# Block attention and expert router on one core: the second product of full expert tiles as seven block products in the two column halves of the array

## The chip, the core and the metric

The kernel runs on one core of a Trainium2 chip. The metric is device time in microseconds (us) of one execution; the lower the better. The engines are called PE (TensorE matmuls; PEld are its weight loads), DVE (VectorE), ACT (ScalarE), POOL (GpSimd) and SP (SyncE, which here issues DMAs).

## What is computed

A block-sparse attention gives x, 3072 rows of 512. Each row goes to the one of 8 experts whose embedding is nearest by cosine, and through that expert's two layers:

```python
N, D, E, F = (3072, 512, 8, 1024)
...
expert_idx = np.argmax(logits, axis=1)
...
for e in range(E):
    mask = expert_idx == e
    ...
    h = np.maximum(x[mask] @ w1[e], 0.0)
    out[mask] = gate_w[mask, None] * (h @ w2[e])
```

Everything is fp32. w1 of an expert is 512 x 1024, w2 1024 x 512: 2 MB each.

## The kernel before

The program has two stages. The first, written in a fixed order, does attention, the logits and most of the routing. The second works through 25 expert tiles of 128 rows (`expert_tiles`, tiles 0 to 24); the change lies in it. The order of instructions in this stage comes from a scheduler that places each engine's instructions from their dependencies and its own estimates of cost; a few places pin an order with `issue_after`. [...]

Tiles 0 to 4 (`NE` is 5) are made of rows that an early dispatch has sorted, the others of rows of the late dispatch. Tiles 11 and 17 are mixed: the upper and the lower 64 rows belong to two experts (`mixed_tile`), so they need two pairs of weights, and each column half of the PE array gets its own. The other 23 tiles are full (`expert_tile`, L1177).

A full tile does this:

- The first product (L1187): hidden features by rows, `h` transposed, in 8 blocks of 128 features, each a sum of 4 matmuls with the weights `w1` stationary and the rows `xt` (128 columns) moving. Blocks 0 to 3 go to PSUM bank `hp0`, blocks 4 to 7 to `hp4`; both have two copies, used in turn by even and odd tiles. An fp32 matmul stands in the profile as two instructions, so the 32 matmuls count 64.
- The relu of `hp0` by ACT (L1190), that of `hp4` by DVE (L1194) into `h`.
- `prepare` of the next tile: for a late tile one DVE transpose (L1168) of the rows fetched, then the gate factor (L1171, L1173); it is pinned to come after the relu (`k.relu`). For tiles 1 to 4 four PE transposes into the bank `xg_ps` and one DVE copy (L1163, L1164).
- The second product (L1200): 8 matmuls with the blocks of `h` stationary and `w2` (512 columns) moving, summed in the bank `yp`.
- `finish`: DVE multiplies `yp` by the gate into `y` (L1212), and POOL scatters `y` to the output rows (L1213). The gathers of a later tile's rows (four per late tile, L1111) are pinned behind that scatter on POOL.

SP loads the weights of each tile afresh (L1140). w1 and w2 have three buffers each; a load into a buffer waits till PE has done with it, so the loads run up to three tiles ahead. In PSUM this stage uses two banks each for `hp0` and `hp4`, one for `yp` and one for `xg_ps`; two more (`small`) serve the dispatch.

Of the kernel before, what the change touches and what calls it, by code (L numbers as in the profile page):

```python
# [16 lines left out]
ALU = mybir.AluOpType  # L17
# [3 lines left out]
P = 128  # L21
# [8 lines left out]
DM, E, F = H * D, 8, 1024  # L30
ND, NF = DM // P, F // P
# [4 lines left out]
HG = G // 2  # L36
# [18 lines left out]
NS = NCH // DUO  # L55
TURNS = [0, 2, 1, 3, *range(4, NCH)]
DEN_LOW, DEN_HIGH = 0.1, 1e10
NEG = -1.0e9
NONE = -30000.0

# [96 lines left out]
def block_mask(k):  # L157
# [16 lines left out]
    both = pool.tile([NB, NB], F32, name="both")  # L174
    nc.vector.tensor_scalar(out=both, in0=m, scalar1=1.0, scalar2=-NEG, op0=ALU.subtract, op1=ALU.mult)
    return both
# [905 lines left out]
def ring(k, name, i, n, pool, shape):  # L1082

    key = name, i % n
    if key not in k.rings:
        k.rings[key] = pool.tile(shape, F32, name=f"{name}_{i % n}")
    return k.rings[key]
# [10 lines left out]
def fetch_rows(k, i):  # L1098

    late = int(i >= NE)  # L1100
    x = ring(k, "xg", i, 4, k.wp2 if i % 4 else k.wp, [P, ND, XE])
    t = ORDER[i - NE] if late else i
    slot = k.slots[late][:, t:t + 1]
    with ExitStack() as order:
        behind = k.scattered if late else None
        if behind is not None:
            order.enter_context(k.tc.issue_after(behind))
        if late:
            quarters = k.x_dram.rearrange("n (e w) -> (n e) w", e=ND)
            for g in range(NG):  # L1110
                k.nc.gpsimd.indirect_dma_start(  # L1111
                    out=x[:, g], out_offset=None, in_=quarters,
                    in_offset=bass.IndirectOffsetOnAxis(ap=k.quarter[:, g, t:t + 1], axis=0),
                    bounds_check=quarters.shape[0] - 1, oob_is_err=False,
                )
        else:
            k.nc.gpsimd.indirect_dma_start(
                out=x.rearrange("p e w -> p (e w)"), out_offset=None, in_=k.x_dram[0:EARLY * S, :],
                in_offset=bass.IndirectOffsetOnAxis(ap=slot, axis=0), bounds_check=EARLY * S - 1, oob_is_err=False,
            )  # L1120
    k.rows[i] = x, slot
# [33 lines left out]
def prepare(k, i):  # L1155

    nc = k.nc
    x, slot = k.rows[i]
    turned = k.turned_rows[i] = ring(k, "xgt", i, 2, k.wp2 if i % 2 else k.wp, [P, ND, P])
    if i < NE:  # L1160
        ps = ring(k, "xg_ps", i, 1, k.eps, [P, ND, P])
        for d in range(ND):
            nc.tensor.transpose(ps[:, d, :], x[:, d, 0:P], k.ident)  # L1163
        nc.vector.tensor_copy(out=turned, in_=ps)  # L1164
        k.rows[i] = x[:, 0, P:XE], slot
        return
    with k.tc.issue_after(k.relu) if k.relu is not None else ExitStack():
        nc.vector.transpose(out=turned.rearrange("p d (g t) -> p d g t", g=NG),  # L1168
                            in_=x[:, :, 0:P].rearrange("p g (t d) -> p d g t", d=ND))
        own = ring(k, "own", i, 2, k.wp2, [P, NG])  # L1170
        nc.vector.tensor_tensor(out=own, in0=x[:, :, P], in1=k.mine, op=ALU.mult)  # L1171
        gate = ring(k, "gate", i, 3, k.wp2, [P, 1])
        nc.vector.reduce_sum(out=gate, in_=own, axis=AX.X)  # L1173
    k.rows[i] = gate, slot


def expert_tile(k, i, meanwhile=None, halfway=None, then=None):  # L1177
    nc = k.nc
    ((w1, w2),), (gate, slot) = k.weights.pop(i), k.rows.pop(i)
    xt = k.turned_rows.pop(i)  # L1180
    h = ring(k, "h", i, 2, k.wp2, [P, NF, P])
    half = NF // 2
    for f0 in (0, half):
        hp = ring(k, f"hp{f0}", i, 2, k.hps, [P, half, P])
        for f in range(half):
            for d in range(ND):
                nc.tensor.matmul(hp[:, f, :], lhsT=w1[:, d, (f0 + f) * P:(f0 + f + 1) * P], rhs=xt[:, d, :],  # L1187
                                 start=(d == 0), stop=(d == ND - 1))
        if f0 == 0:
            nc.scalar.activation(h[:, 0:half], hp, ACT.Relu)  # L1190
            if meanwhile:
                meanwhile()
        else:
            k.relu = nc.vector.tensor_scalar(out=h[:, half:NF], in0=hp, scalar1=0.0, scalar2=None, op0=ALU.max).ins  # L1194

    if i + 1 < k.stop:
        prepare(k, i + 1)
    yp = ring(k, "yp", i, 1, k.eps, [P, DM])
    for f in range(NF):
        nc.tensor.matmul(yp, lhsT=h[:, f, :], rhs=w2[:, f, :], start=(f == 0), stop=(f == NF - 1))  # L1200
        if f == half - 1 and halfway:
            halfway()
    if then:
        then()
    finish(k, i, yp, gate, slot)


def finish(k, i, yp, gate, slot):

    nc = k.nc  # L1210
    y = ring(k, "y", i, 2, k.wp2, [P, DM])
    nc.vector.tensor_scalar(out=y, in0=yp, scalar1=gate, scalar2=None, op0=ALU.mult)  # L1212
    k.scattered = nc.gpsimd.indirect_dma_start(  # L1213
        out=k.out[:, :], out_offset=bass.IndirectOffsetOnAxis(ap=slot, axis=0),
        in_=y[:, :], in_offset=None, bounds_check=N - 1, oob_is_err=False,
    ).ins


def mixed_tile(k, i):
# [29 lines left out]
    for f in range(NF):  # L1249
        for s, (_, w2) in enumerate(weights):  # L1250
            lanes = slice(HG * s, HG * (s + 1))
            nc.tensor.matmul(yp[lanes, :], lhsT=h[:, f, lanes], rhs=w2[:, f, :], start=(f == 0), stop=(f == NF - 1))  # L1252
    finish(k, i, yp, gate, slot)


# [279 lines left out]
def fast(n):  # L1535
    n.rings, n.loads = {}, 0
    with ExitStack() as ctx:
        def pool(name, bufs, **kw):
            return ctx.enter_context(n.tc.tile_pool(name=name, bufs=bufs, **kw))

        n.small, n.eps = pool("small", 1, space=PSUM), pool("eps", 1, space=PSUM)
        n.xp, n.rp, n.xt_pool = pool("xp", 3), pool("rp", 2), pool("xt", 2)
        n.wp_ctx = ctx
        with ExitStack() as attn:
            n.attending = True
            with n.tc.manual_schedule(engines=None):
                attention_fast(n, attn)
            n.attending = False
        n.dp = pool("dp", 1, reuse_waits="tile")
        n.wp2, n.hps = pool("wp2", 1, reuse_waits="tile"), pool("hps", 1, space=PSUM)  # L1550

        def last_rank():
            rank(n, B - 1)
            n.late = dispatch_late(n)
            next(n.late)

        def between():
            yield
            yield
            next(n.late)  # L1560
            count_good(n)
            yield

        def last_route():
            last_logits(n, NCH - 1)
            with n.tc.issue_after(n.relu):
                for _ in route(n, NS - 1):
                    pass

        for _ in n.first_weights:  # L1570
            pass
        for steps in n.unwritten:
            for _ in steps:
                pass
        fetch_rows(n, 1)
        expert_tiles(n, between(), partial(turn_x, n, NCH - 1), last_route, last_rank, lambda: next(n.late))


def more(n):
# [41 lines left out]
@with_exitstack  # L1621
def kernel(
    ctx: ExitStack,
    tc: tile.TileContext,
    q: bass.AP,
    k: bass.AP,
    v: bass.AP,
    sampled_blocks: bass.AP,
    moe_expert_emb: bass.AP,
    moe_tau: bass.AP,  # L1630
    moe_w1: bass.AP,
    moe_w2: bass.AP,
    out: bass.AP,
):
    assert tuple(q.shape) == (B, H, S, D) and tuple(out.shape) == (N, DM)
    assert tuple(moe_w1.shape) == (E, DM, F) and tuple(sampled_blocks.shape) == (NB, NRAND)
    n = Net()
    n.tc, n.nc = tc, tc.nc
    n.q, n.k, n.v, n.blocks, n.out = q, k, v, sampled_blocks, out
    n.emb, n.tau, n.w1, n.w2 = moe_expert_emb, moe_tau, moe_w1, moe_w2  # L1640
    n.loaded, n.vs, n.es, n.ets, n.sums, n.x, n.rows, n.weights = {}, {}, {}, {}, {}, {}, {}, {}

    n.raw, n.nsq, n.lg, n.turned_rows, n.relu = {}, {}, {}, {}, None
    n.kt, n.qt, n.kg, n.pac, n.pd, n.pb, n.av, n.xt = ({} for _ in range(8))
    n.exact = n.attending = False
    n.const = ctx.enter_context(tc.tile_pool(name="const", bufs=1))
    n.x_dram = tc.dram_tile([N + 1, XW], F32, name="x_dram")
    n.dens = n.const.tile([P, NCH, H], F32, name="dens")

    fast(n)  # L1650
    todo = n.nc.values_load(n.todo[0:1, 0:1], min_val=0, max_val=2)
    with tc.If(todo > 0):
        more(n)
# [32 lines left out]
```

## Time and profile before

| | |
|---|---|
| three runs | 632.02, 627.16, 631.42 us; median 631.42 |
| the profiled execution | 626.4 us, its span 624.7 us |
| clock granted to PE in it, mean | 0.986 |
| start of the first expert tile's matmuls | 257.1 us into the span |
| DMA: moved, mean rate | 170.58 MB, 273 GB/s |
| weight loads of the second stage | 52 of 2048 KB, 8 of 512 KB |

The profile is of one execution. Its page gives each engine's busy time and share of the span, the chain of waits that ended last (followed back from the last instruction), and groups of instructions by line: engine, operation, output<-input, shape, count, then busy us and the mean ns of one, then the engine's idle time before them and who ended it. Matmuls overlap in the array, so the mean duration of one is longer than the time from one to the next, and their ends are modelled. The groups of the second product and the scatter:

```profile
L1200 PE MATMUL yp<-w,h 128*128 128x512 f32 x368 | 161.9, 592 | 0.0
L1213 POOL DMA_INDIRECT out_dram<-y,slot_l x20 | 20.4, 1022 | 156.0 <-DVE y L1212 156.0
L1212 DVE TENSOR_SCALAR y<-yp,gate 128x512 f32<-128x512 f32 x20 | 15.0, 751 | 82.0 <-PE yp L1200 69.9
```

### The profile page before, as it was taken

The page shows a single profiled execution, that of the slowest core. Times are in us where ns is not written, and L with a number is a line of the kernel's source. Part 1 is how long each engine was busy: PE and PEld are TensorE (multiplying, and loading weights), DVE is VectorE, ACT ScalarE, POOL GpSimd, SP SyncE. Part 2 cuts the span into 40 slices and gives each one's busy share as a digit, 9 for nine tenths or more (in the row PEclk, how much of TensorE's full clock was granted, in tenths as well). Part 3 has the DMA queues.
Part 4 walks back from the last instruction along what each step waited for, and adds up shares of the span by engine and source line. Part 5 has one row for each costly group of instructions (what it writes and reads, how often), then busy time and mean ns, then how long its engine had stood idle before and what let it go on. Part 6 is the DMA issues. An engine that isn't in the chain of part 4 may idle for free.

```text
span 624.7 us, 18708 instructions
## 1 busy us (share of the span) xinstructions
PE 591.9 (95%) x7678; PEld 454.1 (73%) x7678; DVE 236.1 (38%) x745; ACT 148.0 (24%) x309; POOL 244.1 (39%) x474
## 2 busy tenths in 40 slices
PE   6789998989999997999999999999999999999995
PEld 3678887878888886967777667765777646777772
DVE  2636565676778853239212211212111221111110
ACT  1435555655656653200000000000000000000000
POOL 2626464555766430320243333343333333333432
PEclk9789999999999999999999999999999999999998
DMA  9889888999987971599999999998999998999611
GB/s 167 171 184 193 180 174 180 195 195 208 202 183 186 190 222 37 179 372 399 399 407 398 393 397 365 333 318 305 385 408 398 396 381 308 400 394 410 241 35 34
DMA packets 187312, 170.58 MB, mean 273 GB/s; under 512 B 147720, under 2 KB 147848, under 8 KB 184402
## 3 DMA queue, kind: packets, MB, share of 16 engines
q1 hardware_dynamic: 179906, 155.35, 80.2%
q0 software_dynamic: 5216, 13.43, 5.9%
q8 instruction: 62, 1.02, 0.7%
q10 hardware_dynamic: 2096, 0.52, 0.5%
q14 instruction: 32, 0.26, 0.1%
HBM read 156.65 MB, written 12.90 MB: 271 GB/s over the span
## 4 chain that ended last, share of the span: by engine, by line
PE 82%; ACT 5%; DMA 3%; DVE 2%; issue 2%; POOL 1%; SPq 0%; DVEq 0%; POOLq 0%; ACTq 0%
PE hp L1187 25%; PE yp L1200 24%; PE av L646 8%; PE dps L591 6%; PE ac L566 3%; PE ac L569 3%; PE hp L1232 2%; PE yp L1252 2%; DMA w<-in_moe_w_dram 2%; ACT st L458 2%; ACT pd L596 2%; PE xg_ps L723 2%; PE yp L530 1%; PE xg_ps L752 1%; ACT pb L624 1%
## 5 line engine op out<-in xcount | busy, mean ns | idle before, releaser
L1187 PEld LDWEIGHTS hp<-xgt,w 128*128 128x128 f32 x1472 | 167.8, 192 | 11.9 <-issue 10.2
L1187 PE MATMUL hp<-xgt,w 128*128 128x128 f32 x1472 | 169.2, 276 | 1.4 <-DMA w<-in_moe_w_dram 1.4
L1200 PE MATMUL yp<-w,h 128*128 128x512 f32 x368 | 161.9, 592 | 0.0
L1200 PEld LDWEIGHTS yp<-w,h 128*128 128x128 f32 x368 | 68.1, 190 | 76.5 <-issue 75.7
L1111 POOL DMA_INDIRECT xg<-x_dram,quarter x88 | 89.2, 1014 | 32.3 <-issue 27.4
L1213 POOL DMA_INDIRECT out_dram<-y,slot_l x20 | 20.4, 1022 | 156.0 <-DVE y L1212 156.0
L1190 ACT ACTIVATE h<-hp 128x512 f32<-128x512 f32 x23 | 13.7, 597 | 284.7 <-PE hp L1187 253.8
L1194 DVE TENSOR_SCALAR h<-hp 128x512 f32<-128x512 f32 x23 | 15.9, 691 | 148.5 <-PE hp L1187 148.5
L506 POOL COPY vg<-vt 32x1040 f32<-32x1040 f32 (+1 forms) x45 | 42.8, 952 | 45.6 <-PE av L646 34.4
L548 POOL COPY kg<-kt 128x128 f32 x176 | 43.7, 296 | 35.1 <-ACT kt L519 31.1
L591 PEld LDWEIGHTS dps<-qt,kg 128*64 128x64 f32 x1408 | 47.2, 140 | 3.4 <-issue 3.4
L591 PE MATMUL dps<-qt,kg 128*64 128x64 f32 x1408 | 46.3, 224 | 3.2 <-DVE kg L548 3.2
L566 PE MATMUL ac<-qt,kt 128*64 128x128 f32 x352 | 43.9, 277 | 3.0 <-DVE qt L535 2.7
L1212 DVE TENSOR_SCALAR y<-yp,gate 128x512 f32<-128x512 f32 x20 | 15.0, 751 | 82.0 <-PE yp L1200 69.9
L569 PE MATMUL ac<-qt,kt 128*64 128x256 f32 (+1 forms) x192 | 43.2, 368 | 0.9 <-ACT kt L522 0.9
L566 PEld LDWEIGHTS ac<-qt,kt 128*64 128x64 f32 x352 | 37.8, 137 | 4.2 <-issue 3.2
L535 DVE COPY qt<-yp 64x512 f32<-64x512 f32 x48 | 33.0, 688 | 20.7 <-PE yp L530 20.4
L596 ACT ACTIVATE pd<-dps,bias 128x256 f32<-128x256 f32 x88 | 34.7, 474 | 17.9 <-PE dps L591 17.9
L646 PE MATMUL av<-st,pac 128*64 128x65 f32 x704 | 31.2, 226 | 4.1 <-DVE x L841 3.4
L646 PEld LDWEIGHTS av<-st,pac 128*64 128x64 f32 x704 | 25.6, 138 | 8.6 <-issue 7.6
L646 PE MATMUL av<-vg,pd 128*32 128x65 f32 x1408 | 30.0, 225 | 1.8 <-issue 1.8
L725 DVE COPY xt<-xg_ps 128x512 f32<-128x512 f32 x24 | 16.6, 691 | 35.6 <-PE xg_ps L723 35.6
(240 smaller groups left out, 617.3 us busy)
## 6 DMA issues: line engine op xcount, KB each, us to landing
w<-in_moe_w_dram SPq DMA_DIRECT2D x52, 2048.0 KB
vg<-in_v_dram SPq DMA_DIRECT2D x132, 128.0 KB
kraw<-in_k_dram SPq DMA_DIRECT2D x32, 192.0 KB
x_dram<-x SPq DMA_DIRECT2D x10, 516.0 KB
qraw<-in_q_dram SPq DMA_DIRECT2D x9, 512.0 KB
w<-in_moe_w_dram SPq DMA_DIRECT2D x8, 512.0 KB
vt<-in_v_dram SPq DMA_DIRECT2D x10, 256.0 KB
vt<-in_v_dram SPq DMA_DIRECT2D x5, 512.0 KB
```

Source lines behind the costliest of these rows:

```text
L506: k.nc.gpsimd.tensor_copy(out=k.vg_ring[s % 2][lanes_of(NRAND, g), g, which(i)], in_=k.vt[m][rows, which(i)])
L535: k.nc.vector.tensor_copy(out=t[rows, :, h], in_=ps[rows])
L548: copy(out=t[:, :, g, lanes_of(s, g)], in_=kt[:, :, bass.ds(shift, BLK)])
L566: nc.tensor.matmul(out[0:D, j, half], lhsT=kt[:, j, at:at + D], rhs=qt[:, j, :, D * half:D * (half + 1)], start=True, stop=True)
L569: nc.tensor.matmul(out[D:P, j, half:2].rearrange("p f h t -> p h f t"), lhsT=kt[:, j, S:S + D], rhs=qt[:, j, :, D * half:P].rearrange("p h ...
L591: nc.tensor.matmul(out[D * r:D * (r + 1), NG * j + g], lhsT=kg[:, j, g, D * r:D * (r + 1)], rhs=qt[:, j, :, cols], start=True, stop=True)
L596: nc.scalar.activation(e[:, :, g].rearrange("p j h t -> p j (h t)"), out.rearrange("p (j g) h t -> p j g (h t)", g=NG)[:, :, g], ACT.Exp, ...
L646: k.nc.tensor.matmul(av[lanes, h // NPAIR, h % NPAIR * P:h % NPAIR * P + D + 1], lhsT=lhsT, rhs=rhs, start=first[0], stop=last, skip_group ...
L1111: k.nc.gpsimd.indirect_dma_start(out=x[:, g], out_offset=None, in_=quarters, in_offset=bass.IndirectOffsetOnAxis(ap=k.quarter[:, g, t:t + ...
L1187: nc.tensor.matmul(hp[:, f, :], lhsT=w1[:, d, (f0 + f) * P:(f0 + f + 1) * P], rhs=xt[:, d, :], start=(d == 0), stop=(d == ND - 1))
L1200: nc.tensor.matmul(yp, lhsT=h[:, f, :], rhs=w2[:, f, :], start=(f == 0), stop=(f == NF - 1))
L1213: k.scattered = nc.gpsimd.indirect_dma_start(out=k.out[:, :], out_offset=bass.IndirectOffsetOnAxis(ap=slot, axis=0), in_=y[:, :], in_offse ...
```

## The change

For the full tiles from 3 on, except the last (24), the second product is done by a form of Strassen's identity. The 128 rows of the tile are cut into top and low (64 each), the 1024 features into two halves, the 512 outputs into left and right. The product of two 2 x 2 block matrices is then seven products of blocks, p1 to p7, instead of eight. Each is 64 rows by 256 outputs, a sum over 4 blocks of 128 features, and occupies one column half of the array: p1, p2, p5 the lower-numbered half, p7, p4, p6 the other, in the pairs (p1, p7), (p5, p6), (p2, p4); p3 is cut in two sums over 2 blocks each, one in each half.

The blocks that go in are sums: `sums_of_weights` forms t1 to t4 of w2 on DVE (four operations of 128 x 1024; t1 is written over a part of w2 itself), and `expert_tile` s1 to s4 of h (`hsums`, four of 128 x 256). The results are put together from PSUM by DVE adds of 64 x 256 (u, v, w and parts of y), one such add on POOL, and ACT copies of p1 and p5 into both partition halves; the gate is applied by two ACT multiplies. For the products' outputs the change uses the banks `hp0` and `hp4` of the other parity, which the next tile's first product will write, and `yp` and `xg_ps`. The scatter gets a function of its own.

```diff
@@ -55,6 +55,7 @@
 NS = NCH // DUO
 TURNS = [0, 2, 1, 3, *range(4, NCH)]
 DEN_LOW, DEN_HIGH = 0.1, 1e10
+FIRST_SUMS = 3
 NEG = -1.0e9
 NONE = -30000.0
 
@@ -1174,12 +1175,81 @@
     k.rows[i] = gate, slot
 
 
+def sums_of_weights(k, i, w2):
+
+    nc, half = k.nc, NF // 2
+    left, right = slice(0, DM // 2), slice(DM // 2, DM)
+    t2, t3, t4 = (ring(k, f"wsum{j}", 0, 1, k.wp2, [P, half, DM // 2]) for j in (2, 3, 4))
+    nc.vector.tensor_tensor(out=t3, in0=w2[:, half:NF, right], in1=w2[:, 0:half, right], op=ALU.subtract)
+    t1 = w2[:, 0:half, right]
+    nc.vector.tensor_tensor(out=t1, in0=t1, in1=w2[:, 0:half, left], op=ALU.subtract)
+    nc.vector.tensor_tensor(out=t2, in0=w2[:, half:NF, right], in1=t1, op=ALU.subtract)
+    nc.vector.tensor_tensor(out=t4, in0=w2[:, half:NF, left], in1=t2, op=ALU.subtract)
+    return t1, t2, t3, t4
+
+
+def seven_products(k, i, h, w2, wsums, hsums, gate, slot):
+
+    nc, half = k.nc, NF // 2
+    top, low = slice(0, HG), slice(HG, P)
+    left, right = slice(0, DM // 2), slice(DM // 2, DM)
+    t1, t2, t3, t4 = wsums
+    s1, s2, s3, s4 = hsums
+    spare = [ring(k, f"hp{f0}", i + 1, 2, k.hps, [P, half, P]).rearrange("p f t -> p (f t)") for f0 in (0, half)]
+    yp = ring(k, "yp", i, 1, k.eps, [P, DM])
+    other = ring(k, "xg_ps", i, 1, k.eps, [P, ND, P]).rearrange("p d t -> p (d t)")
+    p1, p2, p5, p3 = spare[0][top, left], spare[0][top, right], yp[top, left], yp[top, right]
+    p7, p4, p6, p3_low = spare[1][low, left], spare[1][low, right], other[low, left], other[low, right]
+    r1, r5, u, v, w = (ring(k, f"part{j}", 0, 1, k.wp2, [P, DM // 2]) for j in range(5))
+    y = ring(k, "y", i, 2, k.wp2, [P, DM])
+
+    def product(f, steps, *pairs):
+        for to, x, wt in pairs:
+            nc.tensor.matmul(to, lhsT=x[:, f], rhs=wt[:, f], start=f == steps[0], stop=f == steps[-1])
+
+    def both(*pairs):
+        for f in range(half):
+            product(f, range(half), *pairs)
+
+    def add(out, one, two, engine=nc.vector):
+        engine.tensor_tensor(out=out, in0=one, in1=two, op=ALU.add)
+
+    h11, h12, h22 = h[:, 0:half, top], h[:, half:NF, top], h[:, half:NF, low]
+    w11, w21, w22 = w2[:, 0:half, left], w2[:, half:NF, left], w2[:, half:NF, right]
+    both((p1, h11, w11), (p7, s3, t3))
+    nc.scalar.copy(out=r1[low], in_=p1)
+    both((p5, s1, t1), (p6, s2, t2))
+    add(u[low], p6, r1[low])
+    nc.scalar.copy(out=r5[low], in_=p5)
+    add(v[low], p7, u[low])
+    both((p2, h12, w21), (p4, h22, t4))
+    add(y[low, right], v[low], r5[low], nc.gpsimd)
+    for f in range(half // 2):
+        product(f, range(half // 2), (p3, s4, w22))
+        product(f + half // 2, range(half // 2, half), (p3_low, s4, w22))
+    nc.scalar.copy(out=r1[top], in_=p1)
+    nc.scalar.copy(out=r5[top], in_=p5)
+    add(y[top, left], p2, r1[top])
+    add(y[low, left], p4, v[low])
+    nc.scalar.mul(y[low], y[low], gate[low])
+    add(w[top], p3_low, u[low])
+    add(w[top], w[top], r5[top])
+    add(y[top, right], p3, w[top])
+    nc.scalar.mul(y[top], y[top], gate[top])
+    scatter(k, y, slot)
+
+
 def expert_tile(k, i, meanwhile=None, halfway=None, then=None):
     nc = k.nc
     ((w1, w2),), (gate, slot) = k.weights.pop(i), k.rows.pop(i)
     xt = k.turned_rows.pop(i)
     h = ring(k, "h", i, 2, k.wp2, [P, NF, P])
     half = NF // 2
+    fewer = k.fewer and FIRST_SUMS <= i < k.stop - 1
+    if fewer:
+        wsums = sums_of_weights(k, i, w2)
+        hsums = [ring(k, f"hsum{j}", 0, 1, k.wp2, [P, half, HG]) for j in range(1, 5)]
+    top, low = slice(0, HG), slice(HG, P)
     for f0 in (0, half):
         hp = ring(k, f"hp{f0}", i, 2, k.hps, [P, half, P])
         for f in range(half):
@@ -1188,13 +1258,22 @@
                                  start=(d == 0), stop=(d == ND - 1))
         if f0 == 0:
             nc.scalar.activation(h[:, 0:half], hp, ACT.Relu)
+            if fewer:
+                nc.vector.tensor_tensor(out=hsums[2], in0=h[:, 0:half, top], in1=h[:, 0:half, low], op=ALU.subtract)
             if meanwhile:
                 meanwhile()
         else:
             k.relu = nc.vector.tensor_scalar(out=h[:, half:NF], in0=hp, scalar1=0.0, scalar2=None, op0=ALU.max).ins
+    if fewer:
+        nc.vector.tensor_tensor(out=hsums[0], in0=h[:, 0:half, low], in1=h[:, half:NF, low], op=ALU.add)
+        nc.vector.tensor_tensor(out=hsums[1], in0=hsums[0], in1=h[:, 0:half, top], op=ALU.subtract)
+        nc.vector.tensor_tensor(out=hsums[3], in0=h[:, half:NF, top], in1=hsums[1], op=ALU.subtract)
 
     if i + 1 < k.stop:
         prepare(k, i + 1)
+    if fewer:
+        seven_products(k, i, h, w2, wsums, hsums, gate, slot)
+        return
     yp = ring(k, "yp", i, 1, k.eps, [P, DM])
     for f in range(NF):
         nc.tensor.matmul(yp, lhsT=h[:, f, :], rhs=w2[:, f, :], start=(f == 0), stop=(f == NF - 1))
@@ -1210,7 +1289,12 @@
     nc = k.nc
     y = ring(k, "y", i, 2, k.wp2, [P, DM])
     nc.vector.tensor_scalar(out=y, in0=yp, scalar1=gate, scalar2=None, op0=ALU.mult)
-    k.scattered = nc.gpsimd.indirect_dma_start(
+    scatter(k, y, slot)
+
+
+def scatter(k, y, slot):
+
+    k.scattered = k.nc.gpsimd.indirect_dma_start(
         out=k.out[:, :], out_offset=bass.IndirectOffsetOnAxis(ap=slot, axis=0),
         in_=y[:, :], in_offset=None, bounds_check=N - 1, oob_is_err=False,
     ).ins
@@ -1573,7 +1657,9 @@
             for _ in steps:
                 pass
         fetch_rows(n, 1)
+        n.fewer = True
         expert_tiles(n, between(), partial(turn_x, n, NCH - 1), last_route, last_rank, lambda: next(n.late))
+        n.fewer = False
 
 
 def more(n):
@@ -1642,7 +1728,7 @@
 
     n.raw, n.nsq, n.lg, n.turned_rows, n.relu = {}, {}, {}, {}, None
     n.kt, n.qt, n.kg, n.pac, n.pd, n.pb, n.av, n.xt = ({} for _ in range(8))
-    n.exact = n.attending = False
+    n.exact = n.attending = n.fewer = False
     n.const = ctx.enter_context(tc.tile_pool(name="const", bufs=1))
     n.x_dram = tc.dram_tile([N + 1, XW], F32, name="x_dram")
     n.dens = n.const.tile([P, NCH, H], F32, name="dens")
```

## The prediction

> **What bounds the kernel now.** I read the engines' busy time first, then the chain of waits, then the groups, then single tiles.
>
> ```profile
> PE 591.9 (95%) x7678; PEld 454.1 (73%) x7678; DVE 236.1 (38%) x745; ACT 148.0 (24%) x309; POOL 244.1 (39%) x474
> ...
> PE hp L1187 25%; PE yp L1200 24%; PE av L646 8%; PE dps L591 6%; PE ac L566 3%; PE ac L569 3%; PE hp L1232 2%; PE yp L1252 2%; DMA w<-in_moe_w_dram 2%; ACT st L458 2%; ACT pd L596 2%; PE xg_ps L723 2%; PE yp L530 1%; PE xg_ps L752 1%; ACT pb L624 1%
> ```
>
> Half the span is the two products of the full expert tiles, on PE. The merged chain (start us, us, what) shows that stage, here one full tile, then the mixed tile:
>
> ```profile
> 404.30 7.14 PE hp L1187 x64
> 411.45 6.87 PE yp L1200 x16
> 418.32 7.07 PE hp L1232 x32
> 425.39 0.59 PE hp L1244 x4
> 425.97 0.20 issue
> 426.17 0.66 PE hp L1244 x4
> 426.82 7.02 PE yp L1252 x32
> 433.84 7.34 PE hp L1187 x64
> ```
>
> A full tile takes 7.14 + 6.87 = 14.01 us, and PE never waits. The second product is 16 instructions (8 steps, each in two passes) of 512 columns, 0.429 us each. The mixed tile drives each column half of the array with its own weights: 32 instructions in 7.02 us, so two halves run at once, a pair each 0.43 us. Going into and out of that form costs something: 7.02 against 6.87, and 7.34 against 7.14 for the product after it. In a full tile PE is busy 14.02 of 14.02 us, DVE only 2.65:
>
> ```profile
> 362.26:376.28 14.02, 14.02 (x83) 10.20 (x82) 2.65 (x5) 0.60 (x1) 5.08 (x5) 1.00 1.02 394
> ```
>
> The timeline of one tile shows when DVE gets to work behind the first product:
>
> ```profile
> 341.22 7.03 PE L1200 MATMUL yp<-w,h 128*128 128x512 f32 x16
> ...
> 342.65 0.69 DVE L1194 TENSOR_SCALAR h<-hp 128x512 f32<-128x512 f32 x1 [7.63 <-PE hp L1187]
> ...
> 343.26 1.09 DVE L1168 STREAM_TRANSPOSE xgt<-xg 128x512 f32<-128x512 f32 x1
> ...
> 344.28 0.12 DVE L1171 TENSOR_TENSOR own<-xg,mine 128x4 f32<-128x4 f32 x1
> ```
>
> The first product's last matmul ends at about 341.38 in this trace, yet the relu of its second half starts 1.27 us later. In the last tile, where nothing queues behind the second product, it starts 0.04 us after. I call this delay the lag. It costs nothing now, since PE needs that half 3.4 us into the second product.
>
> Durations that the change will use:
>
> ```profile
> L1168 DVE STREAM_TRANSPOSE xgt<-xg 128x512 f32<-128x512 f32 x20 | 21.9, 1094 | 0.0
> ...
> L708 DVE TENSOR_TENSOR x<-av,inv 64x256 f32<-64x256 f32 x4 | 1.7, 422 | 0.1
> ...
> L927 DVE TENSOR_TENSOR ge<-ge 128x576 f32<-128x576 f32 x1 | 0.8, 751 | 0.0
> ...
> L765 DVE TENSOR_TENSOR good_lo<-good_lo,good_hi 128x192 f32<-128x192 f32 x1 | 0.4, 359 | 0.0
> ```
>
> [...]
>
> **The change part by part.** It applies to tiles 3 to 23 but for the mixed ones (11 and 17): 19 tiles. I count from E, the slot end of the first product's last matmul. [...]the changed program's own listing gives order and waits.
>
> PE arithmetic. Out: 16 x 0.429 = 6.87 us. In: seven products of 4 steps x 2 passes of 256 columns. Six run in pairs, the seventh split over both halves: 14 steps x 2 x 0.2147 (half of 0.429) = 6.01 us. Gain 0.86; the mode changes take back 0.35 (the two differences above). Left alone that is -0.5 us a tile.
>
> First wait. The first pair (p1, p7) ends at E + 0.14 + 1.72 = 1.86. The second needs s1 and s2. DVE's order is relu, transpose of the next tile's rows, s1, own, s2. Relu starts at E + 0.22 + lag (0.18 remainder of the last matmul, 0.04 wake-up); 0.61 and 1.02 to the next two starts (timeline above); 0.42 + 0.04 + 0.42 for s1 and s2; about 0.1 to PE: p6 starts at E + 2.8 + lag. The lag has not been seen behind 256-column pairs; bounds 0 (last tile) and 1.2 (full tiles), less than 0 being excluded. I take 0.3, as these followers leave the queue four times as fast as the 512-column ones, and 0.65 as a plausible high end. So E + 3.05, a stall of 1.2 us. All ten steps left for the upper half come after it.
>
> Second wait. p6 ends 1.8 later, 4.87. p4 goes to the bank and quadrants that p7 lies in; the listing has p4 wait for DVE's v, which reads p7 and needs u, which needs p6 complete. Completion 0.2 plus 0.15 lag, u 0.42, v 0.46, wake-up 0.1: p4 starts at about 6.2. Three of p2's four steps fill part of that, but they are in the lower half; the upper stands idle 1.3 us. p4 1.72 to 7.94, p3 0.86 to 8.80.
>
> Third wait. The next tile's first product reuses the banks of p1, p2, p4, p7, so it waits for two adds after p4: 7.94 + 0.3 + 0.42 + 0.42 + 0.06 = 9.1. p3, the mode change and one matmul that needs only the first add end at 9.1 too, so nothing to little is lost (cover: p3; without it 0.9).
>
> Sum: the next first product starts at E + 9.0 instead of 6.87: **+2.1 us a tile**, 19 x 2.15 = 41 us. With no lag 1.67 a tile, 32 us; with 0.65, 2.8 a tile, 53 us.
>
> Other work. DVE gains 4 x 1.22 (weight sums) + 4 x 0.42 (s) + 7 x 0.42 (adds) and loses 0.75 (y): 2.65 becomes about 11.5 of 16.1 us. The weight sums sit under the first product: the tail adds of the tile before end about 1 us into it, the sums at 5.9, s3 at 6.5, against a relu due at 7.3: hidden, with 0.6 to 0.8 to spare. They need w2 at the tile's start instead of its middle; landings in the trace are 3 us or more ahead (after the mixed tiles the least), except perhaps for tile 3, once. ACT gets four copies (0.26 to 0.59 each, rows of 128x128 and 128x512) and two multiplies of 0.6 on 0.60: idle enough; the third copy holds the last add till p2 is done, beside the first add. POOL gets one add of 0.3 to 0.6 us (copies of 128x128 and 32x520) on 5.08; the scatter comes some 2 us later and the row gathers behind it with it, under a tile and more of slack. SP issues the same loads; w2's release now waits for DVE and PE both, later by what the tile grows. The loads need about 10.5 us of DMA a tile at 400 GB/s, less than either tile time.
>
> **Rivals.** (A) The above: the dependent chain PE-DVE-PE is exposed twice a tile. 626.4 + 41 = 667. (B) Faster: the exposed waits stay below the 0.5 us that the arithmetic leaves, place: p6 and p4. With none the tile is 13.5, 19 x -0.5 = -10: 617. For it: DVE is idle 11.4 of 14 us now. Against it: relu, transpose, s1 and s2 are 2.5 us from rows in the trace, and p1/p7 cover 1.7. It decides below 0.5 us of waits; I find 2.6. (C) DVE becomes the bound: if a weight sum takes 1.6 us rather than 1.22 (POOL's five DMA issues of 1.0 us lie beside them), its spare is gone and relu slips 0.7 a tile, 681; at 2.0 it is 2.3 us a tile, 710. (D) p4's wait proves short, as if v were ready: only the first wait and the mode change remain, about +0.8 a tile, 642. (E) The halves do not run at once: 28 steps x 0.429 = 12.0 us, 5.1 more a tile, 724; the mixed tile speaks against it.
>
> **Numbers.** The sum stands against the profiled execution, 626.4 us (span 624.7); the runs shown are 627.16 to 632.02, median 631.42, 5 above it. I add 3: **670 us**. Chances: A 0.73, B 0.07, C 0.12, D 0.06, E 0.02. A spans 658 to 680 and 5 more for the median; taking in the mild end of C and leaving out B, D, E and the heavy end of C gives 652 to 692. A measurement tells 1% (6.3 us) here. Faster 0.04 and same 0.03 are B, its clean and its half-covered form; slower 0.93.
>
> **What would show it.** In the profile after: full tiles of about 16.1 us; the 256-column matmuls in pairs 0.215 us apart; the idle time of PE (or its weight loads) before p6 ended by DVE's s2, about 1.2 us, and before p4 by v; relu's start 0.05 to 0.7 us past the first product's end; weight sums at 1.22 us; no wait on w. I am wrong if PE has no such idle time (B), if relu starts over a us late behind DVE's own queue (C), or if only p6 waits (D).

## The result, and the profile after

The changed kernel took 681.05 us, the median of 4 runs (678.55 to 681.82); the kernel before, on the same chip, 629.79 (627.16 to 632.02). The ratio is 1.081, with a 95% interval of 1.075 to 1.087. The profiled execution took 681.8 us, its span is 680.1, 55.4 longer than before.

The page of the changed kernel, its engines and the chain of waits that ended last:

```profile
PE 624.8 (92%) x8438; PEld 490.3 (72%) x8438; DVE 394.5 (58%) x1011; ACT 202.1 (30%) x423; POOL 277.6 (41%) x493
...
PE 59%; DVE 9%; issue 8%; DMA 7%; ACT 6%; POOL 5%; SPq 1%; POOLq 0%; DVEq 0%; ACTq 0%
```

PE's share of the chain fell from 82% to 59%; DVE, DMA, ACT and POOL, which had 2%, 3%, 5% and 1%, took its place. PE's busy time even grew by 33 us: one column half at work counts as a busy PE while the other waits (in the tile that begins at 379.59 below, matmuls of p2 keep PE busy from 391.51 to 392.75 while p4 waits). Here busy time says little, the chain more.

Full tiles now come in two kinds. The view of engines by stretch (length, then busy us and instructions of PE, PEld, DVE, ACT, POOL, then clock, DMA share, GB/s) for one of each:

```profile
379.59:395.74 16.15, 15.30 (x122) 11.81 (x121) 11.38 (x20) 3.29 (x7) 6.14 (x6) 1.00 0.82 293
362.07:379.59 17.52, 15.94 (x121) 11.99 (x121) 10.91 (x20) 3.58 (x8) 7.53 (x7) 1.00 0.74 270
```

Of the 18 tiles from 4 on that the change touches, nine take 15.8 to 16.2 us and nine 16.6 to 17.6. The first kind, in the timeline of the tile that begins at 379.59 (E, as in the forecast, is where the slot of its first product's last matmul ends: 386.84):

```profile
387.04 0.69 DVE L1266 TENSOR_SCALAR h<-hp 128x512 f32<-128x512 f32 x1 [0.46 <-PE hp L1257]
387.65 1.47 DVE L1169 STREAM_TRANSPOSE xgt<-xg 128x512 f32<-128x512 f32 x1
...
389.46 0.43 DVE L1269 TENSOR_TENSOR hsum<-hsum,h 128x256 f32<-128x256 f32 x1
...
389.94 0.43 PE L1208 MATMUL xg_ps<-wsum,hsum 128*64 128x256 f32 x1
...
391.99 0.43 DVE L1215 TENSOR_TENSOR part<-xg_ps,part 64x256 f32<-64x256 f32 x1 [1.64 <-ACT part L1223]
392.52 0.43 DVE L1215 TENSOR_TENSOR part<-hp,part 64x256 f32<-64x256 f32 x1
393.00 0.86 PE L1208 MATMUL hp<-wsum,h 128*64 128x256 f32 x3 [0.25 <-DVE part L1215]
```

These are the two stalls of the forecast. p6 (into `xg_ps`) starts at E + 3.10, at once behind s2, where the pair before it ended at E + 1.87. p4 starts at E + 6.16, at once behind v, the second of the two adds. The next first product starts at 395.74, E + 8.90.

Six of the nine tiles of the second kind have a third stall that the forecast didn't have (the other three are accounted for in the section on the prediction). The timeline of the tile that begins at 362.07, its first product already running:

```profile
363.43 0.72 POOL L1215 TENSOR_TENSOR y<-part,part 64x256 f32<-64x256 f32 x1 [6.33 <-DMA xg<-x_dram,quarter]
364.18 0.72 ACT L1234 ACTIVATE y<-y,gate 64x512 f32<-64x512 f32 x1 [2.85 <-POOL y L1215]
364.92 0.36 ACT L1231 COPY part<-yp 64x256 f32<-64x256 f32 x1
365.32 0.42 DVE L1215 TENSOR_TENSOR part<-part,part 64x256 f32<-64x256 f32 x1 [2.67 <-ACT part L1231]
...
370.16 1.21 DVE L1187 TENSOR_TENSOR wsum<-w,wsum 128x1024 f32<-128x1024 f32 x1
...
371.30 0.68 DVE L1266 TENSOR_SCALAR h<-hp 128x512 f32<-128x512 f32 x1
```

These are leftovers of the tile before. POOL's add of y[low, right] stands behind the four row gathers on POOL, and its list of waits names their semaphores, though it reads nothing that they bring (why the list has them is not shown): it waits till they have landed (6.33 us). ACT's gate multiply needs that add; the copy of p5 to r5[top] is listed behind the multiply and starts at its end, 364.92, though PE's last matmul into `yp` had ended at 361.34; DVE's adds of w need that copy; the four weight sums are behind those; and the relu, due at E + 0.2 (369.5), starts at 371.30. The waits of the whole run (who waited for whom: us in total, times, longest) have the same links:

```profile
POOL y L1215 <- DMA xg<-x_dram,quarter: 83.6, 18, 6.6
ACT y L1234 <- POOL y L1215: 26.4, 12, 3.2
DVE part L1215 <- ACT part L1231: 19.8, 12, 2.8
```

Where the 55.4 us lie, from the starts of the tiles' first matmuls in the two profiled executions: before tile 0, 3.1; tiles 0 to 2, 2.6; tile 3, 3.1; tiles 4 to 23, 46.2; the end, 0.4. A second profiled execution of the changed kernel (below) gives -0.6, 2.6, 3.1, 45.5 and 0.3: the first term is scatter of the first stage, the others repeat, though of the 2.6 not all comes from the list of instructions (see the section on the prediction). So from here on I compare, beside the time, the stretch from tile 4's first matmul to that of tile 24, which this scatter doesn't touch: 283.7 us in the kernel before, 329.9 and 329.2 in the changed one.

### The profile page after: what moved, and what is told of

Its sections match the earlier page's. It is cut to its first block, busy times and chain, and to the rows that moved or that the text cites. A ratio compares the mean times of both kernels' runs of the same rounds, so it can differ in the third digit from the quotient of the medians.

```text
span 680.1 us, 20834 instructions
## 1 busy us (share of the span) xinstructions
PE 624.8 (92%) x8438; PEld 490.3 (72%) x8438; DVE 394.5 (58%) x1011; ACT 202.1 (30%) x423; POOL 277.6 (41%) x493
## 4 chain that ended last, share of the span: by engine, by line
PE 59%; DVE 9%; issue 8%; DMA 7%; ACT 6%; POOL 5%; SPq 1%; POOLq 0%; DVEq 0%; ACTq 0%
PE hp L1257 15%; PE av L647 6%; PE hp L1208 6%; PE dps L592 6%; DMA xg<-x_dram,quarter 5%; PE xg_ps L1208 4%; PE ac L567 3%; PE yp L1279 3%; POOL xg L1112 3%; PE ac L570 2%; PE hp L1316 2%; PE yp L1336 2%; DVE part L1215 2%; PE yp L1208 2%; ACT pd L597 2%
## 5 line engine op out<-in xcount | busy, mean ns | idle before, releaser
L1112 POOL DMA_INDIRECT xg<-x_dram,quarter x88 | 97.7, 1110 | 32.3 <-issue 27.7
L1208 PE MATMUL hp<-w,h 128*64 128x256 f32 x304 | 77.8, 386 | 2.9 <-ACT part L1220 2.9
L1208 PE MATMUL yp<-w,hsum 128*64 128x256 f32 x228 | 57.4, 386 | 10.1 <-DVE hsum L1268 6.4
L1297 POOL DMA_INDIRECT out_dram<-y,slot_l x20 | 29.8, 1491 | 89.4 <-ACT h L1260 38.4
L1208 PEld LDWEIGHTS hp<-w,h 128*64 128x64 f32 x304 | 38.0, 136 | 18.5 <-ACT part L1220 4.7
L1215 POOL TENSOR_TENSOR y<-part,part 64x256 f32<-64x256 f32 x19 | 14.9, 784 | 89.2 <-DMA xg<-x_dram,quarter 83.6
L1208 PE MATMUL hp<-wsum,h 128*64 128x256 f32 x152 | 36.9, 385 | 5.3 <-DVE part L1215 5.0
L1208 PEld LDWEIGHTS yp<-w,hsum 128*64 128x64 f32 x228 | 25.6, 136 | 18.7 <-DVE hsum L1268 10.4
L1215 DVE TENSOR_TENSOR y<-hp,part 64x256 f32<-64x256 f32 x38 | 16.1, 422 | 37.9 <-PE hp L1208 29.2
L1208 PE MATMUL hp<-wsum,hsum 128*64 128x256 f32 x152 | 36.9, 385 | 1.0 <-DVE hsum L1262 0.9
L726 DVE COPY xt<-xg_ps 128x512 f32<-128x512 f32 x24 | 16.6, 691 | 36.6 <-PE xg_ps L724 36.6
```

What stands on the lines that cost most here:

```text
L1112: k.nc.gpsimd.indirect_dma_start(out=x[:, g], out_offset=None, in_=quarters, in_offset=bass.IndirectOffsetOnAxis(ap=k.quarter[:, g, t:t + ...
L1208: nc.tensor.matmul(to, lhsT=x[:, f], rhs=wt[:, f], start=f == steps[0], stop=f == steps[-1])
L1215: engine.tensor_tensor(out=out, in0=one, in1=two, op=ALU.add)
```

## The experiments

| kernel | median, us | ratio to before, 95% | tiles 4 to 23, us |
|---|---|---|---|
| changed (again) | 679.95 | 1.087 (1.081 to 1.092) | 329.2 |
| copy_first | 674.43 | 1.080 (1.074 to 1.085) | 323.0 |
| add_on_dve | 673.89 | 1.077 (1.074 to 1.081) | 324.2 |
| sums_first | 670.44 | 1.073 (1.069 to 1.078) | 322.0 |
| dve_sums_first | 660.27 | 1.054 (1.050 to 1.058) | 310.3 |
| dve_bank | 647.41 | 1.033 (1.028 to 1.037) | 298.8 |
| all_three | 634.84 | 1.011 (1.008 to 1.015) | 286.5 |
| raw_weights | 632.62 | 1.010 (1.007 to 1.012) | - |
| tidied | 627.54 | 0.999 (0.997 to 1.002) | 280.0 |
| trimmed | 624.29 | 0.994 (0.991 to 0.996) | 277.3 |
| no_sums | 620.04 | 0.988 (0.984 to 0.992) | 274.9 |

### Is it POOL's add, and through which link?

copy_first cuts the chain at ACT and leaves POOL's add as it is:

```diff
-    nc.scalar.copy(out=r5[top], in_=p5)
+    last = nc.scalar.copy(out=r5[top], in_=p5).ins
...
-    nc.scalar.mul(y[low], y[low], gate[low])
+    with k.tc.issue_after(last):
+        nc.scalar.mul(y[low], y[low], gate[low])
```

> Edit: on ACT the copy of p5 into r5[top] is pinned ahead of the gate multiply of y[low]; POOL's add stays. Theory (ACT's queue passes POOL's lateness on): in seven tiles of the changed kernel POOL's add, which waits for its own row gathers to land, comes after the next first product has begun; the multiply waits for it, the copy behind the multiply, DVE's last adds for the copy, the weight sums and the relu behind those. With the copy ahead, DVE never waits for POOL there: relu at the first product's end + 0.2 us in all tiles but the two after the mixed ones, tiles of 16.1 us, in all -6 us against the changed kernel: 675 (671 to 678). POOL's add is as late as before. Rival (DVE's own load makes the relu late): no change, 681. Rival (a late POOL add stops DVE through the buffers v and y): no change.

The stretch fell by 6.2 to 6.9 us. POOL's add is late as before, and no longer matters. The timeline of its tile that begins at 502.72:

```profile
503.40 0.42 DVE L1215 TENSOR_TENSOR part<-part,part 64x256 f32<-64x256 f32 x1
...
505.02 0.97 POOL L1215 TENSOR_TENSOR y<-part,part 64x256 f32<-64x256 f32 x1 [5.98 <-DMA xg<-x_dram,quarter]
505.44 1.64 DVE L1185 TENSOR_TENSOR w<-w 128x1024 f32<-128x1024 f32 x1
...
510.17 0.69 DVE L1267 TENSOR_SCALAR h<-hp 128x512 f32<-128x512 f32 x1 [0.36 <-PE hp L1258]
```

POOL's add comes 2.3 us into the first product, later than in the bad tile above, yet DVE's add of w is done by then and the relu is on time, waiting for PE. In the time of the whole program, each kernel against the kernel before on its own chip, the gain is 3 to 5 us and the intervals overlap; the stretch tells.

add_on_dve takes the add from POOL altogether:

```diff
-    add(y[low, right], v[low], r5[low], nc.gpsimd)
+    add(y[low, right], v[low], r5[low])
```

> Edit: the add of y[low, right] from POOL to DVE, nothing else. Theory (POOL's wait for its gathers starts the chain): no wait of the sort is left, relu at the first product's end + 0.2 us but for the tiles after the mixed ones, tiles of 16.1 us, -6 us against the changed kernel: 675 (670 to 678), the scatters earlier too. Rival (DVE's load): one add of 0.42 us more on DVE in 19 tiles, so no gain or up to 8 us slower, 681 to 689.

The stretch fell by 5.0 to 5.7 us, about as much, though DVE has one add more. On DVE the add's list names one DMA semaphore, that of the scatter which last read its `y`, where on POOL it named five. So the chain POOL, ACT, DVE is the cause of the third stall, with ACT's order as its link, and the rival, DVE's load, is refuted. Not all went as expected: in four tiles the relu is still 0.3 to 0.4 us late though DVE is free, and in two p4 starts 0.9 late; both belong to the late completions shown below.

### The first stall

sums_first moves the transpose of the next tile's rows behind s2, by what it is pinned to:

```diff
-        nc.vector.tensor_tensor(out=hsums[1], in0=hsums[0], in1=h[:, 0:half, top], op=ALU.subtract)
+        k.relu = nc.vector.tensor_tensor(out=hsums[1], in0=hsums[0], in1=h[:, 0:half, top], op=ALU.subtract).ins
```

> Edit: the transpose of the next tile's rows is pinned behind s2 instead of behind the relu. p6 then starts some 1.1 us earlier after the first product's end (3.07 becomes 1.95). Theory (gathers, POOL's add, ACT, scatter and the next gathers form a loop of about 16.5 us a tile): the stall before p6 goes, yet most of it comes back as a late relu in more tiles than now; 670 to 681, gain below 11 us. Rival (the two PE-DVE waits alone set the tile): 19 x -1.1 = -20 us, 661 (657 to 665).

dve_sums_first does this and takes the add to DVE.

> Edit: both of the two before: the add of y[low, right] on DVE and the transpose behind s2. Theory: without the loop the earlier p6 counts in full: tiles of 15.0 us, 675 - 20 = 655 (650 to 660). Rival (no loop): the same as with the transpose moved alone, within 4 us or the same distance apart as the add alone makes.

sums_first alone gained 7.2 to 7.9 us on the stretch, not 20. Together with the add on DVE, it gained 13.8 more than that add alone. So the first stall's price depends on the chain: the two stalls had partly hidden one another. In the waits of sums_first the chain's links have grown with what was taken from the stall:

```profile
ACT y L1234 <- POOL y L1215: 38.0, 15, 4.1
DVE part L1215 <- ACT part L1231: 29.5, 15, 3.9
```

In dve_sums_first p6 starts at E + 1.9 to 2.3 in 15 of the 18 tiles. Ten of these take 14.85 to 15.23 us, as expected. In the other five p4 starts 1.1 to 2.1 late and they take 15.7 to 16.7; over add_on_dve they gained 1.0 us together, and that is most of why 13.8 was less than 20. (Tile 4 and the two after the mixed ones, where p6 starts later, take 16.0.) The timeline of the worst:

```profile
433.22 0.38 PE L1208 MATMUL xg_ps<-wsum,hsum 128*64 128x256 f32 x1
433.39 1.46 PE L1208 MATMUL hp<-w,h 128*64 128x256 f32 x6
...
435.74 0.36 ACT L1223 COPY part<-yp 64x256 f32<-64x256 f32 x1 [3.29 <-remote]
435.80 0.43 DVE L1215 TENSOR_TENSOR part<-xg_ps,part 64x256 f32<-64x256 f32 x1 [2.55 <-remote]
...
436.75 0.65 PE L1208 MATMUL hp<-wsum,h 128*64 128x256 f32 x2 [1.90 <-DVE part L1215]
```

p6's last matmul ends at 433.60 by its record, but ACT and DVE, both free, see p5 and p6 complete only at 435.7. In most tiles u, the first of the two adds, starts 0.11 us behind p6's recorded end, here 2.2 us. This is the same kind of delay as the lag of the forecast, in another place.

### The second stall

dve_bank has the add on DVE and gives p4 a bank of its own, one of the two of `small` that the dispatch no longer needs:

```diff
-    p7, p4, p6, p3_low = spare[1][low, left], spare[1][low, right], other[low, left], other[low, right]
+    if ("p4", 0) not in k.rings:
+        k.rings["p4", 0] = two_banks(k, "p4")[:, 0]
+    p4 = k.rings["p4", 0][low, right]
+    p7, p6, p3_low = spare[1][low, left], other[low, left], other[low, right]
```

The changed kernel ran once more beside it:

> The changed kernel as it is, beside the next three on one chip. It should stand to the kernel before as it did (ratio 1.075 to 1.087), with tiles that alternate between 16.1 us and 16.6 to 17.6, and some 330 us from the first matmul of tile 4 to that of tile 24 (284 in the kernel before).

It did, with a ratio of 1.087 and 329.2 us on the stretch. For dve_bank:

> Edit: the add of y[low, right] on DVE as before, and p4 in a PSUM bank of its own (one of the two that the dispatch has given up), so that it needn't wait for v. Theory (the wait of p4 for v is on the path): p4 starts where p6 ends, a tile loses 1.35 us against the add alone, 18 x -1.35 = -24 us: 300 us (297 to 306) from tile 4 to tile 24 where the add alone gave 324, and 649 in all (645 to 655). Rival (p4's wait is covered, as what counts is the last add before the next first product): less than 5 us.

The stretch fell by 25.3 us against add_on_dve, 1.4 a tile. In the timeline of a tile, p6 (into `xg_ps`) is followed at once by p4 (into `p`), before v:

```profile
380.86 0.38 PE L1211 MATMUL xg_ps<-wsum,hsum 128*64 128x256 f32 x1
...
381.07 0.38 PE L1211 MATMUL p<-wsum,h 128*64 128x256 f32 x1
...
381.80 0.43 DVE L1218 TENSOR_TENSOR part<-hp,part 64x256 f32<-64x256 f32 x1
```

This tile took 16.05 us in add_on_dve and takes 14.82. The mean gain is larger, as in tile 4 and the two after the mixed ones (1.9 to 2.1 each) PE's list now has p4 ahead of p6, and as two late completions are gone. The wait came from the shared bank alone; no data of p4 hangs on v.

all_three joins the three edits.

> Edits: the add on DVE, the transpose behind s2, the bank for p4. Theory (these three were the whole loss): tiles near the arithmetic, 7.25 + 6.4 = 13.65 us, 280 to 292 us from tile 4 to tile 24 (kernel before: 284), 626 to 638 in all. Rival (DVE, busy some 12 us a tile, becomes the bound at that tile time, or the late completions of matmuls that appeared where PE has few waits stand in for the waits removed): 293 or more, 639 to 650.

286.5 us, within the theory's range: most full tiles take 13.6 to 14.1. raw_weights asks whether the weight sums still cost something there.

```diff
-    t2, t3, t4 = (ring(k, f"wsum{j}", 0, 1, k.wp2, [P, half, DM // 2]) for j in (2, 3, 4))
...
+    t1, t2 = w2[:, 0:half, right], w2[:, half:NF, right]
+    t3, t4 = w2[:, 0:half, left], w2[:, half:NF, left]
```

> As the last one, but the four sums of w2 are left out: t1 to t4 are blocks of w2 itself, so the output is not the product. DVE has 4.9 us a tile less to do. If DVE's load costs time in the last kernel, this one is faster by it; its floor by PE's arithmetic is 18 x 13.65 + 2 x 15.6 = 277 us from tile 4 to tile 24. If the weight sums are hidden there, within 3 us of it.

2 us faster, the intervals overlap: by the time, they are hidden or nearly so. Its one profile is of its slowest execution (638.9 us), so its tiles say nothing here.

### What is left of the form

tidied keeps the three edits, puts the copy first on ACT, pins s3 behind the weight sums (after a mixed tile it stood second among them and waited 2.5 us for ACT's relu, with the sums behind it) and begins with tile 4:

```diff
-FIRST_SUMS = 3
+FIRST_SUMS = 4
...
+                with k.tc.issue_after(k.summed):
+                    nc.vector.tensor_tensor(out=hsums[2], in0=h[:, 0:half, top], in1=h[:, 0:half, low],
+                                            op=ALU.subtract)
```

(`k.summed` is the fourth weight sum.)

> The last correct one (add on DVE, transpose behind s2, bank for p4) with three more edits: the copy of p5 ahead of the gate multiply on ACT, s3 pinned behind the four weight sums so that it can't hold them up after a mixed tile, and tile 3 done as before the change (the seven products begin with tile 4). Theory: the two tiles after the mixed ones lose their late relu (14.7 becomes 13.6 to 13.9 us), the tiles whose relu was 0.6 late come to 13.6, tile 3 is 1.4 shorter: 277 to 283 us from tile 4 to tile 24, 625 to 632 in all, about equal to the kernel before. Rival (late completions of matmuls, seen in the last two kernels where PE hardly waits, put the time back): 285 or more, 633 to 637.

trimmed leaves out the tiles after the mixed ones as well:

```diff
-    fewer = k.fewer and FIRST_SUMS <= i < k.stop - 1
+    fewer = k.fewer and FIRST_SUMS <= i < k.stop - 1 and len(parts(i - 1)) == 1
```

> As tidied, but the two tiles that follow the mixed ones are done as before the change: 16 tiles with the seven products. In tidied these two took 14.9 us against 14.0, as their sums can't begin before the mixed tile has ended. Theory: 2 x -0.9 = -1.9 us, 278 us from tile 4 to tile 24, 625.5 in all, a ratio to the kernel before of 0.996 (0.992 to 0.999). Rival: the tiles behind those (14.0 in tidied) now lag in their place, no change against tidied, ratio 1.000.

no_sums puts plain blocks of h and w2 in place of the eight sums of tidied:

```diff
+        hsums = [h[:, half:NF, low], h[:, half:NF, top], h[:, 0:half, low], h[:, half:NF, top]]
```

> As tidied, but all eight sums that go into the products are left out: the blocks of h and of w2 take their place, so the output is not the product; the adds behind the products stay. It asks what the form could give if its sums cost nothing. By PE's arithmetic a tile is 13.6 us, 276 us from tile 4 to tile 24 against 284 in the kernel before: about -8 us there and, with some 2.6 that tiles 0 to 2 lose through the other order of instructions, 619 to 625. Rival (late completions of matmuls put a stall in place of each one removed): 285 or more, 628 or more.

tidied equals the kernel before, as expected: tiles of 13.57 us where no special case applies, 280.0 on the stretch. Of the 3.7 gained there, tiles 0 to 3 take back 1.0; the rest is within the scatter of the first stage. The two tiles after mixed ones still took 14.9, which the theory missed: their relu was on time, but PE's list there has p4 ahead of p6, so the halves fall out of step: in the one behind tile 11 the half of p1 starts no matmul between 444.67 and 446.24 (read from the trace; no run changes that order alone). trimmed is the one correct kernel here that is faster than the kernel before, by 0.65% (0.4 to 0.9). The stretches of one full tile, first in trimmed, then in no_sums:

```profile
352.31:365.89 13.58, 13.58 (x123) 11.86 (x121) 11.69 (x21) 3.50 (x7) 5.20 (x5) 1.00 1.02 390
```

```profile
349.42:362.95 13.53, 13.53 (x122) 11.15 (x121) 5.20 (x13) 3.50 (x7) 5.07 (x5) 1.00 1.04 403
```

DVE is busy 11.69 of 13.58 us and PE never waits: with all sums free a tile is only 0.05 us shorter. So 0.5 us a tile is what the form can give here, 8.8 us in 18 tiles; in the changed kernel the waits cost 55 us (329.9 less 274.9), and 46 of loss is what remained.

## Why the prediction was right, and which terms were off

The sum of the forecast was 667 for the profiled execution, which took 681.8; with its 3 us more, 670 for the median, which was 681. The sign and the main mechanism, rival A, were right; the size fell short by 11 to 15. Of the 15, about 8 are costs that the sum put at nothing for tiles 3 to 23, 2.6 lie in tiles 0 to 2, and 3.5 are the scatter of the first stage and the end.

- **Arithmetic, -0.5 a tile.** Right: no_sums has 13.53 against 14.02.
- **First wait.** p6 was put at E + 3.05 (its own terms, with the lag, add up to 3.13); it starts at 3.07 to 3.13 in seven of the nine tiles without the third stall, at 2.75 in the other two. That it came so close is luck, as two errors cancelled inside: the lag of 0.3, the author's estimate, wasn't there (the relu starts at E + 0.20), and from the transpose to s1 it took 1.39 us in the tile shown, not 1.02 (the transposes' mean rose from 1094 to 1210 ns).
- **Second wait.** p4 was put at E + 6.2; mostly 6.13 to 6.19. Its price of 1.3 us measured 1.2 with the bank in an ordinary tile, 1.4 on the mean. Why the shared bank needs the order that the listing gives was not shown; the runs show what it costs.
- **Third wait.** The next first product was put at E + 9.0: mostly 8.87 to 8.93. A tile of 16.1 was right for half of the tiles.
- **The two costs set at nothing that weren't.** "POOL gets one add ... on 5.08", with slack behind it, was the step that failed. Its time was priced (0.3 to 0.6; it took 0.72), the waits in its list were not: it stands behind its own engine's gathers and waits for them to land. ACT "idle enough" was as wrong for the same reason: ACT had the time, but the copy was queued behind a late multiply. And the cover of the weight sums, "hidden, with 0.6 to 0.8 to spare", held only while the adds before them were on time. In tiles 4 to 23, counted over the 16.14 us of an ordinary tile, the chain cost 6.0 us in six tiles, s3 among the sums 1.5 in the two after mixed tiles, and a weight sum listed between relu and s1 0.9 in tile 4.
- **Tile 3.** The same sort: 3.1 us instead of 2.15; there one weight sum stands between relu and s1, and another between s1 and s2.
- **Tiles 0 to 2** were not in the sum, as the change doesn't touch them. They lost 2.6 us in both profiled executions, but 1.6 of it goes with the clock, not with the list of instructions: the clock granted to PE in tile 1 was 0.89 there and 1.00 in the kernel before, and tile 1 took 15.7 us. In copy_first, whose list of instructions is the same up to there and whose clock in tile 1 was 1.00, that tile took 14.1 and the three lost 1.0. That much goes with the other order of instructions: the scheduler put two of POOL's row gathers in among its routing adds, and tile 0's relu, behind the same routing on DVE, starts 1.3 us later than before. No run isolates this.
- **DVE's load**, 11.5 of 16.1 forecast, is 11.38 of 16.15; the weight sums take 1.21 to 1.23. The forecast's 1.22 was an estimate; the prediction's rows of 192 and 576 columns (359 and 751 ns), carried on in a straight line to 1024, give 1.21. Rival C's price for a weight sum didn't come, though its sign did: the relu started over 1 us late behind DVE's own queue in seven of the 18 tiles, from other causes. That C's 681 is the time measured is chance. Rivals B, D and E fell: both waits are exposed (1.23 us before p6 and 1.2 to 1.4 before p4), and the halves run side by side (in the tile shown p1 and p7 start at 386.93 and 386.94, and later pairs follow 0.21 to 0.22 apart).

The 41 us of the sum became 49 through terms that stood at zero and lay on other engines' queues; of those on the PE and DVE path, each start came within 0.15 us in most tiles without such a cost.

## What to carry to other kernels

Fewer multiplications pay only what PE gains per tile, here 0.5 us, and each hand-over PE, DVE, PE in the middle of a tile cost 1.2 to 1.4 us where no other PE work and no other bank covered it, and p4's own bank took 25.3 us off the stretch; so place outputs in banks by who reads what when, before counting products. An operation given to a "free" engine inherits that engine's queue: look at what stands before it there and what that waits for, then at who is queued behind its consumer. And when two stalls share a loop, taking one away shows less than it cost; take both.

## What the runs showed of the hardware that was not expected

- What follows does not by itself decide the lag. Behind 256-column pairs DVE starts the relu 0.04 us after the first product's recorded end in the tile shown of the changed kernel (387.00 and 387.04), where it was 1.27 behind the 512-column matmuls. But behind the same pairs u started 1.2 to 2.3 us after p6's recorded end in five tiles of dve_sums_first and three of all_three, 0.5 to 1.0 in some of sums_first, add_on_dve and dve_bank, and 0.11 in all but one tile of each of tidied and trimmed. What sets it stays open.
- DVE and POOL at work beside each other took longer, on either side. In copy_first a weight sum that began while POOL's add was under way (505.44, in the timeline above) took 1.64 us instead of 1.22; in other tiles the sum kept 1.21 and the add took up to 1.98 instead of 0.72. In the changed kernel an add that began 0.20 us behind the start of a sum took 1.60, the sum 1.22.
- POOL's scatters took longer too, and their time went with what was left of the weight sum under way when they began. In the changed kernel, with 0.8 us left, they took 1.66 to 1.75 us, with 0.52 left 1.41, against 1.02 in the kernel before; in add_on_dve most began 0.1 us before the end of a sum and took 1.02, though the next sum ran beside them. In the changed kernel the sums beside them stayed at 1.21 to 1.23, so POOL alone paid; in no_sums, without the sums, all took 1.02 to 1.03.
